# Pooled attention followed by a GELU MLP: the first group in halves, later exps, and the loads on another DMA queue

## The chip, the cores and the metric

The kernel runs on one core of a Trainium2 chip. The metric is the device time of one execution in microseconds (us), lower is better. Engines are named as in the profile: PE (TensorE, matmuls), DVE (VectorE), ACT (ScalarE), POOL (GpSimd) and SP (SyncE, which here only issues DMAs); PEld are the weight loads of PE. The granted clock is the share of PE's full clock that the profile shows as granted. A core has 16 DMA engines; both SP and ACT can issue DMAs, each on a queue of its own.

Executions of a program come in two states, fast and slow. Medians are over all runs. A ratio is the mean time of one kernel's fast runs over that of the other's of the same rounds, so it is not quite the ratio of the medians quoted beside it.

## The reference

```python
# q, k, v: [8 batches, 8 heads, 576 tokens, 64]
k_p = k.reshape(B, H, 72, 8, D).mean(axis=3)      # pooled: 576 keys become 72
v_p = v.reshape(B, H, 72, 8, D).mean(axis=3)
attn = softmax(q @ k_p.T / sqrt(D))
x = (attn @ v_p) as [8*576 tokens, 512]
out = gelu_tanh(x @ w_in) @ w_out                 # w_in [512, 2048], w_out [2048, 512]
```

## The kernel before

The 4608 tokens are nine groups of 512: the first 512 tokens of each of the eight batches, and one group of the 64 tokens left over in each (called R). For each group the MLP is 64 matmuls into the hidden layer and 64 out of it, 512 columns each. The attention of the *next* group is hung into this stream by hooks: `at(s, f)` emits `f` ahead of matmul `s` (0 to 63 hidden, 64 to 127 output). A hook fixes only the order on each engine. An engine that has nothing earlier to do runs its part as soon as its inputs are there.

A steady group (g is the group whose MLP runs, n the next, and the loads are for the one after):

```python
at(0,   pool, dup_k, k_transpose_dma, cast_q, q_transpose_dma)   # DVE, POOL, and DMA transposes on SP's queue
at(30,  loads, seq[n_ + 2])                                      # 3.4 MB of k, v, q, on SP's queue
at(60, 62, 78, 81, scores, n, j)                                 # 4 matmuls and one exp on ACT each
at(79, 81, 85, 89, norm, n, j)                                   # DVE sum, 1/sum; product eb on DVE or POOL
at(79, 81, 85, 89, e_transpose_dma, n, j)                        # eT <- eb, a DMA transpose on SP's queue
at(120, preload gelu table, values, n)                           # 8 matmuls on eT and vbd; ACT copies xT
```

The first group has nothing to hide behind. Its order is: pool K, scores, all four norms, pool V, spread V into the block matrix `vbd` on DVE, PE transposes of the probabilities, values, xT copies, and only then the MLP. The casts of `w_in` run on POOL meanwhile:

```python
norm(0, 3, nc.gpsimd)
pool(0, 5, 9)                    # V, after the softmax
pool(0, 0, 1, 0, 64)
spread_v(0, nc.vector)
[...]
for c in range(4):
    cast_w_in(c, nc.gpsimd)
```

The softmax here doesn't subtract the row's maximum and nothing guards it: scores larger than these inputs give would overflow.

## Time and profile before

| | |
|---|---|
| time | 340.75 us median of 3 (340.33 to 341.77); 341.14 of 4 with the later round |
| span in the profile | 339.6 us |
| first MLP matmul | 37.6 us |
| first MLP matmul of group 1 | 86.7 us |
| from there to the next group's | 31.3, 30.9, 31.2, 31.8, 33.6, 31.4, 30.8 us |

The group starts are read from the timeline of PE: the first matmul that reads `w_in_b` in each group. Two facts set up the argument: before 86.7 us PE idles a lot; after it, the groups follow at about 31 us and PE hardly idles. The prediction below shows the lines. One more view is needed later, the timeline of SP's DMA queue in a steady group (start, length of the issue, queue, line, operation), because the order in it turned out to carry the kernel:

```profile
93.89 1.80 SPq L183 DMA_TRANSPOSE qT<-q_b  x1
95.74 1.14 SPq L97 DMA_DIRECT2D kv<-in_k_dram  x1
...
98.71 0.60 SPq L105 DMA_DIRECT2D q_sb<-in_q_dram  x1
104.72 1.21 SPq L224 DMA_TRANSPOSE eT<-eb  x1
...
108.74 4.26 SPq L224 DMA_TRANSPOSE eT<-eb  x3
```

One queue issues in order: the transpose of q, then the loads, then the transposes of the softmax. The order does not keep them wholly apart: the load of q issued here at 98.71 lands at 109.9, and the four transposes of the softmax land 5.8, 3.1, 2.6 and 2.6 us after their issue. But the last of them, for which the values must wait, meets no load any more, and after group 1's start PE waits for these transposes 1.1 us in all.

### The profile page before, as it was taken

How to read it: one execution, taken by the hardware profiler on the slowest of the kernel's cores; microseconds unless marked ns; L12 is line 12 of the kernel's file. 1: busy time of each engine (PE TensorE's matmuls, PEld its weight loads, DVE VectorE, ACT ScalarE, POOL GpSimd, SP SyncE). 2: the span in 40 equal slices, each digit the busy share in tenths (PEclk: the TensorE clock that was granted, in tenths of full speed). 3: DMA queues.
4: the chain of work that ended last, by engine and by line, in shares of the span. 5: the costliest groups of instructions: out<-in, count | busy, mean ns of one | idle time of the engine just before them, and what ended most of it. 6: DMA issues, size and time to landing. Idle time of an engine off the chain costs nothing. (4 is left out here: it accounts for less than half of the span.)

```text
span 339.6 us, 4031 instructions
## 1 busy us (share of the span) xinstructions
PE 292.8 (86%) x1545; PEld 140.8 (41%) x1545; DVE 133.4 (39%) x193; ACT 171.1 (50%) x237; POOL 73.3 (22%) x68
## 2 busy tenths in 40 slices
PE   5511999092999999999999998999699999999995
PEld 4411544040444444444444443444244454444442
DVE  5488109270606262642446071616162510340011
ACT  1430762040678268446836772685268546926600
POOL 2097225422111320402041113202220400020000
PEclk9555899787899999999999999999999999999999
DMA  7981994599099429926980997299426333162011
GB/s 236 347 313 27 347 348 178 113 315 225 32 236 294 124 65 286 266 102 129 340 187 31 221 283 150 63 296 194 135 72 166 91 122 52 21 129 53 2 62 62
DMA packets 74643, 56.99 MB, mean 168 GB/s; under 512 B 48512, under 2 KB 56704, under 8 KB 74624
## 3 DMA queue, kind: packets, MB, share of 16 engines
q1 hardware_dynamic: 74544, 56.60, 62.5%
q8 instruction: 12, 0.20, 0.2%
q10 hardware_dynamic: 80, 0.13, 0.1%
q14 instruction: 7, 0.06, 0.1%
HBM read 36.70 MB, written 9.44 MB: 136 GB/s over the span
## 5 line engine op out<-in xcount | busy, mean ns | idle before, releaser
L283 PE MATMUL mm<-w_out_b,gT 128*128 128x512 bf16 x576 | 132.5, 382 | 1.6 <-ACT gT L273 1.5
L271 PE MATMUL mm<-xT,w_in_b 128*128 128x512 bf16 x576 | 128.6, 380 | 0.5 <-ACT xT L77 0.5
L273 ACT ACTIVATE gT<-mm 128x512 bf16<-128x512 f32 x144 | 85.9, 597 | 45.2 <-PE mm L271 45.0
L283 PEld LDWEIGHTS <-gT 128*128 128x128 bf16 x576 | 55.7, 98 | 67.5 <-ACT gT L273 3.5
L271 PEld LDWEIGHTS <-w_in_b 128*128 128x128 bf16 x576 | 55.8, 98 | 66.1 <-issue 2.0
L287 DVE COPY osb<-mm 128x512 f32<-128x512 f32 x36 | 24.6, 687 | 92.0 <-PE mm L283 92.0
L211 POOL TENSOR_TENSOR eb<-e,r 128x576 bf16<-128x576 f32 x20 | 23.9, 1198 | 140.0 <-DVE r L210 100.6
L208 DVE TENSOR_REDUCE den<-e 128x8 f32<-128x576 f32 x36 | 26.6, 739 | 66.3 <-ACT e L201 65.5
L77 ACT CAST xT<-xo 128x1024 bf16<-128x1024 f32 x16 | 15.5, 1014 | 48.9 <-PE xo L242 43.8
L201 ACT ACTIVATE e<-sc 128x576 f32<-128x576 f32 x36 | 22.6, 650 | 31.2 <-PE sc L192 15.2
L124 DVE TENSOR_TENSOR kv<-kv 128x2304 f32<-128x2304 f32 (+3 forms) x12 | 23.1, 1926 | 15.8 <-DMA kv<-in_v_dram 13.6
L242 PE MATMUL xo<-eT,vbd 128*128 128x512 bf16 x56 | 14.9, 414 | 11.0 <-DMA eT<-eb 8.3
L135 POOL TENSOR_TENSOR vbd<-kvb,vmask 128x768 bf16<-128x768 bf16 x7 | 10.5, 1499 | 62.2 <-DVE kvb L126 62.2
L192 PE MATMUL sc<-kbd,qT 128*128 128x144 bf16 x128 | 14.6, 244 | 8.7 <-DMA qT<-q_b 7.7
L192 PEld LDWEIGHTS <-qT 128*128 128x128 bf16 x128 | 10.9, 105 | 16.4 <-DMA qT<-q_b 8.2
L79 POOL CAST q_b<-q_sb 128x2048 bf16<-128x2048 f32 x8 | 15.6, 1956 | 5.7 <-issue 4.3
L125 DVE TENSOR_TENSOR kv<-kv 128x1152 f32<-128x1152 f32 (+3 forms) x12 | 15.6, 1300 | 0.4
L211 DVE TENSOR_TENSOR eb<-e,r 128x576 bf16<-128x576 f32 x16 | 14.2, 888 | 0.6
L232 PE MATMUL mm<-eT,vbd 128*128 128x128 bf16 x32 | 3.6, 282 | 12.2 <-DVE vbd L138 12.1
L242 PEld LDWEIGHTS <-vbd 128*128 128x128 bf16 x56 | 5.3, 103 | 19.8 <-issue 7.9
L382 POOL CAST w_out_b<-w_out_s 128x2048 bf16<-128x2048 f32 x4 | 8.0, 2012 | 19.3 <-DMA w_out_s<-in_moe_w_out_dram 19.3
L126 DVE TENSOR_TENSOR kvb<-kv 128x576 bf16<-128x576 f32 (+3 forms) x12 | 11.5, 956 | 0.4
(47 smaller groups left out, 112.6 us busy)
## 6 DMA issues: line engine op xcount, KB each, us to landing
kv<-in_v_dram SPq DMA_DIRECT2D x8, 1024.0 KB, 9.4
out_dram<-osb SPq DMA_DIRECT2D x32, 256.0 KB, 2.5
kv<-in_k_dram SPq DMA_DIRECT2D x7, 1024.0 KB, 7.3
q_sb<-in_q_dram SPq DMA_DIRECT2D x7, 1024.0 KB, 11.4
w_in_s<-in_moe_w_in_dram SPq DMA_DIRECT2D x4, 1024.0 KB, 14.0
w_out_s<-in_moe_w_out_dram SPq DMA_DIRECT2D x4, 1024.0 KB, 13.0
kv<-in_k_dram SPq DMA_DIRECT2D x2, 512.0 KB, 5.2
q_sb<-in_q_dram SPq DMA_DIRECT2D x2, 512.0 KB, 7.4
```

The source lines that it names most:

```text
L79: eng.tensor_copy(out=out, in_=in_)
L124: add(out=t[:, :, 0:4, :], in0=t[:, :, 0:4, :], in1=t[:, :, 4:8, :], op=ALU.add)
L125: add(out=t[:, :, 0:2, :], in0=t[:, :, 0:2, :], in1=t[:, :, 2:4, :], op=ALU.add)
L192: nc.tensor.matmul(out=o, lhsT=qT[:, j, pr, :], rhs=kbd[:, g, pr].rearrange("d hh s -> d (hh s)"), start=True, stop=True)
L201: nc.scalar.activation(out=e.rearrange("p (x h) s -> p x (h s)", x=2), in_=sc[:, :, 0:4 * Sp], func=ACT.Exp, scale=1.0 / 64.0)
L208: nc.vector.reduce_sum(out=den, in_=e, axis=AX.X)
L211: eng.tensor_tensor(out=eb[:, j, 0:W].rearrange("p (h s) -> p h s", s=Sp), in0=e, in1=r.unsqueeze(2).to_broadcast([128, H, Sp]), op=ALU.mult)
L242: nc.tensor.matmul(out=xo[:, i, :], lhsT=vbd[:, g, n, :], rhs=eT[:, :, c, :], start=(x == 0), stop=(x == 1))
L271: nc.tensor.matmul(out=hp, lhsT=w_in_b[:, ko, fo * 128:(fo + 1) * 128], rhs=xT[:, ko, :], start=(ko == 0), stop=(ko == KO - 1))
L273: nc.scalar.activation(out=gT[:, fo, :], in_=hp, func=ACT.Gelu_apprx_tanh)
L283: nc.tensor.matmul(out=ops[i], lhsT=gT[:, fo, (r0 + i) * 128:(r0 + i + 1) * 128], rhs=w_out_b[:, fo, :], start=(fo == 0), stop=(fo == FO - 1))
L287: nc.vector.tensor_copy(out=osb, in_=ops[i])
```

## The change

The intent is to start the MLP of group 0 earlier (half of its tokens first, V pooled before the softmax is normalised, each weight block cast just ahead of its use), to prepare group 1 with PE transposes, to put the exps behind the last gelu so that ACT switches its table twice instead of four times a group, and to take the loads off SP's queue so that the transposes there don't stand behind them. The core of the diff, cut:

```diff
-        e = work.tile([128, H, Sp], F32, name="e")
+        st[g][("sc", j)] = sc
+
+    def exps(g, j):
+        sc = st[g].pop(("sc", j))
+        e = work.tile([128, H, Sp], F32, name="e", bufs=4)
[...]
     load_half(0, "k", nc.scalar)
+    load_half(0, "v", nc.scalar)
[...]
-    pool(0, 1, 3)
[...]
+    pool(0, 0, 3)
[...]
+    pool(0, 5, 7)
+    spread_v(0, nc.gpsimd, (0,))
+    pool(0, 7, 9)
+    norm(0, 0, nc.vector)
+    spread_v(0, nc.gpsimd, (1,))
+    norm(0, 1, nc.vector)
[...]
+    values_half(0, 0, [nc.scalar, nc.vector])
     nc.scalar.preload_act_table_set(GELU_SET)
+    cast_w_in(0, nc.vector)
+    norm(0, 2, nc.gpsimd)
+    norm(0, 3, nc.vector)
+    cast_w_in(1, nc.gpsimd)
+    cast_w_in(2, nc.vector)
+    cast_w_in(3, nc.gpsimd)
[...]
+    at(hooks, 178, loads, 2, nc.scalar)       # end of group 0
[...]
-            t0 = 64 if first else 0
+            t0 = 20
[...]
+                at(hooks, [60, 62, 76, 79][j], scores, n, j)
+                at(hooks, [64, 64, 76, 79][j], exps, n, j)
[...]
-            at(30 if n_ else 100, loads, seq[n_ + 2])
+            at(hooks, 92, loads, seq[n_ + 2], nc.scalar)
```

More of the change, by code (lines that the diff above doesn't have):

```diff
@@ L130, in dup_k, with spread_v, kT_tile @@
         nc.vector.tensor_copy(out=kvb[:, c0:c1, 1, :], in_=kvb[:, c0:c1, 0, :])
-    def spread_v(b, eng):
+    def spread_v(b, eng, parts=(7, 0, 1)):
         kvb = st[b]["kvb"]
         mult = eng.tensor_tensor
-        mult(out=vbd[:, b, 1:7, :].rearrange("p (c r) (hh d) -> p c (r hh) d", c=3, d=D),
-             in0=kvb[:, 6:9, 0, :].unsqueeze(2).to_broadcast([128, 3, 4, D]),
-             in1=vmask[:, 1:4, :].unsqueeze(3).to_broadcast([128, 3, 4, D]), op=ALU.mult)
-        mult(out=vbd[:, b, 0, :].rearrange("p (hh d) -> p hh d", d=D),
-             in0=kvb[:, 5:6, 0, :].to_broadcast([128, 2, D]),
-             in1=vmask[:, 0, 2:4].unsqueeze(2).to_broadcast([128, 2, D]), op=ALU.mult)
-        mult(out=vbd[0:64, b, 7, :].rearrange("p (hh d) -> p hh d", d=D),
-             in0=kvb[0:64, 0:1, 0, :].to_broadcast([64, 2, D]),
-             in1=vmask[0:64, 4, 0:2].unsqueeze(2).to_broadcast([64, 2, D]), op=ALU.mult)
-    def kT_tile(b, ps):
-        if ps:
-            st[b]["kT"] = psum.tile([128, 5 * 128], BF16, name="kT", tag="mm", bufs=4)
+        if 7 in parts:
+            mult(out=vbd[0:64, b, 7, :].rearrange("p (hh d) -> p hh d", d=D),
+                 in0=kvb[0:64, 0:1, 0, :].to_broadcast([64, 2, D]),
+                 in1=vmask[0:64, 4, 0:2].unsqueeze(2).to_broadcast([64, 2, D]), op=ALU.mult)
+        if 0 in parts:
+            mult(out=vbd[:, b, 0, :].rearrange("p (hh d) -> p hh d", d=D),
+                 in0=kvb[:, 5:6, 0, :].to_broadcast([128, 2, D]),
+                 in1=vmask[:, 0, 2:4].unsqueeze(2).to_broadcast([128, 2, D]), op=ALU.mult)
+        if 1 in parts:
+            mult(out=vbd[:, b, 1:7, :].rearrange("p (c r) (hh d) -> p c (r hh) d", c=3, d=D),
+                 in0=kvb[:, 6:9, 0, :].unsqueeze(2).to_broadcast([128, 3, 4, D]),
+                 in1=vmask[:, 1:4, :].unsqueeze(3).to_broadcast([128, 3, 4, D]), op=ALU.mult)
+    BUFS = {"mm": 4, "sc": 2}
+    def kT_tile(b, tag):
+        if tag:
+            st[b]["kT"] = psum.tile([128, 5 * 128], BF16, name="kT", tag=tag, bufs=BUFS[tag])
         else:
@@ L169, in qT_tile, with q_transpose_pe @@
         st[g]["qT"] = work.tile([128, 4, HP, 128], BF16, name="qT", bufs=1)
-    def q_transpose_pe(g, half, eng):
-        tp = psum.tile([128, 4, 2, 128], BF16, name="tp", tag="mm", bufs=4)
+    def q_transpose_pe(g, half, eng, tag):
+        tp = psum.tile([128, 4, 2, 128], BF16, name="tp", tag=tag, bufs=BUFS[tag])
         for i in range(2):
@@ L217, in e_transpose_pe @@
     def e_transpose_pe(g, j, eng):
-        tp = psum.tile([128, 5, 128], BF16, name="tp", tag="sc", bufs=2)
+        tp = psum.tile([128, 5, 128], BF16, name="tp", tag="mm", bufs=4)
         for c in range(5):
@@ L227, in xT_tile, with values_half @@
         st[g]["xT"] = work.tile([128, KO, MAIN], BF16, name="xT")
-    def values_block(g, j, xo):
+    def values_half(g, half, engs):
+        xo = psum.tile([128, HP, 256], F32, name="xo", tag="sc", bufs=2)
         for pr in range(HP):
             for i, (c, n) in enumerate(PARTS[pr]):
-                nc.tensor.matmul(out=xo[pr][:, 128 * j:128 * j + 128], lhsT=vbd[:, g, n, :],
-                                 rhs=st[g]["eT"][:, j, c, :], start=(i == 0), stop=(i == 1))
+                nc.tensor.matmul(out=xo[:, pr, :], lhsT=vbd[:, g, n, :],
+                                 rhs=st[g]["eT"][:, 2 * half:2 * half + 2, c, :], start=(i == 0), stop=(i == 1))
+        for x in range(2):
+            copy(engs[x], st[g]["xT"][:, 2 * x:2 * x + 2, 256 * half:256 * half + 256], xo[:, 2 * x:2 * x + 2, :])
     def values(g, half, eng):
@@ L260, in store, with runner @@
                 nc.sync.dma_start(out=out[r0:r0 + 64, :], in_=osb[64 * half:64 * half + 64])
-    def mlp(g, hooks, nr):
+    def runner(hooks):
         def hook(s):
@@ L265, in hook @@
                 f()
-        xT = st[g]["xT"]
-        for fo in range(FO):
-            hp = psum.tile([128, MAIN], F32, name="mm", tag="mm", bufs=4)
-            for ko in range(KO):
-                hook(4 * fo + ko)
-                nc.tensor.matmul(out=hp, lhsT=w_in_b[:, ko, fo * 128:(fo + 1) * 128], rhs=xT[:, ko, :],
-                                 start=(ko == 0), stop=(ko == KO - 1))
-            nc.scalar.activation(out=gT[:, fo, :], in_=hp, func=ACT.Gelu_apprx_tanh)
-            if fo == FO - 1 and hooks:
-                nc.scalar.preload_act_table_set(EXP_SET)
@@ L276, in mlp @@
-        s = 64
-        for r0 in range(0, 4, nr):
-            ops = [psum.tile([128, DM], F32, name="mm", tag="mm", bufs=4) for _ in range(nr)]
-            for fo in range(FO):
-                for i in range(nr):
-                    hook(s)
-                    s += 1
-                    nc.tensor.matmul(out=ops[i], lhsT=gT[:, fo, (r0 + i) * 128:(r0 + i + 1) * 128],
-                                     rhs=w_out_b[:, fo, :], start=(fo == 0), stop=(fo == FO - 1))
-            for i in range(nr):
-                osb = work.tile([128, DM], F32, name="osb", bufs=4)
-                nc.vector.tensor_copy(out=osb, in_=ops[i])
-                store(g, r0 + i, osb)
+        return hook
@@ new lines, in hidden, with output @@
+    def hidden(g, fo, c0, c1, hook, s):
+        hp = psum.tile([128, MAIN], F32, name="mm", tag="mm", bufs=4)
+        for ko in range(KO):
+            hook(s + ko)
+            nc.tensor.matmul(out=hp[:, 0:c1 - c0], lhsT=w_in_b[:, ko, fo * 128:(fo + 1) * 128],
+                             rhs=st[g]["xT"][:, ko, c0:c1], start=(ko == 0), stop=(ko == KO - 1))
+        nc.scalar.activation(out=gT[:, fo, c0:c1], in_=hp[:, 0:c1 - c0], func=ACT.Gelu_apprx_tanh)
+    def output(g, r, fo, o):
+        nc.tensor.matmul(out=o, lhsT=gT[:, fo, r * 128:(r + 1) * 128], rhs=w_out_b[:, fo, :],
+                         start=(fo == 0), stop=(fo == FO - 1))
@@ new lines, in finish, with mlp @@
+    def finish(g, r, o, eng):
+        osb = work.tile([128, DM], F32, name="osb", bufs=4)
+        copy(eng, osb, o)
+        store(g, r, osb)
+    def mlp(g, hooks, last):
+        hook = runner(hooks)
+        for fo in range(FO):
+            hidden(g, fo, 0, MAIN, hook, 4 * fo)
+        if not last:
+            nc.scalar.preload_act_table_set(EXP_SET)
+        for r in range(4):
+            o = psum.tile([128, DM], F32, name="mm", tag="mm", bufs=4)
+            for fo in range(FO):
+                hook(64 + 16 * r + fo)
+                output(g, r, fo, o)
+            finish(g, r, o, nc.vector)
+        assert not hooks, sorted(hooks)
@@ new lines, in mlp_first @@
+    def mlp_first(g, hooks):
+        hook = runner(hooks)
+        s = 0
+        for half, c in [(0, 0), (0, 1), (0, 2), (1, 0), (0, 3), (1, 1), (1, 2), (1, 3)]:
+            for fo in range(4 * c, 4 * c + 4):
+                hidden(g, fo, 256 * half, 256 * half + 256, hook, s)
+                s += 4
+        nc.scalar.preload_act_table_set(EXP_SET)
+        o = [psum.tile([128, DM], F32, name="mm", tag="mm", bufs=4) for _ in range(4)]
+        for fo in range(12):
+            for r in range(4):
+                hook(s)
+                s += 1
+                output(g, r, fo, o[r])
+        for r in range(4):
+            for fo in range(12, FO):
+                hook(s)
+                s += 1
+                output(g, r, fo, o[r])
+            finish(g, r, o[r], nc.scalar if r == 3 else nc.vector)
@@ L300 @@
     load_q(0, 4, 8, nc.sync)
-    load_main(0, "v", 0, 4, nc.sync)
-    load_half(0, "v", nc.sync)
+    load_main(0, "v", 0, 2, nc.sync)
+    load_main(0, "v", 2, 4, nc.sync)
     nc.scalar.preload_act_table_set(EXP_SET)
@@ L315, in cast_w_in, with w_out_load, cast_w_out @@
         copy(eng, w_in_b[:, :, o:o + 512], w_in_s[c // 2][:, :, 512 * (c % 2):512 * (c % 2) + 512])
+    w_out_s = {}
+    def w_out_load(c):
+        if c % 2 == 0:
+            w_out_s[c // 2] = kvp.tile([128, 8, DM], F32, name="w_out_s", tag="kv")
+        t = w_out_s[c // 2][:, 4 * (c % 2):4 * (c % 2) + 4, :]
+        nc.sync.dma_start(out=t, in_=moe_w_out[512 * c:512 * c + 512, :].rearrange("(fo p) c -> p fo c", p=128))
+    def cast_w_out(c, eng):
+        copy(eng, w_out_b[:, 4 * c:4 * c + 4, :], w_out_s[c // 2][:, 4 * (c % 2):4 * (c % 2) + 4, :])
     make_identity(nc, identb)
@@ L325, with warm_up @@
     nc.gpsimd.memset(vbd[64:128, :, 7, :], 0.0)
-    warm = psum.tile([128, MAIN], F32, name="warm", tag="mm", bufs=4)
-    for _ in range(40):
-        nc.tensor.matmul(out=warm[:, 0:128], lhsT=identb, rhs=identb, start=True, stop=True)
-    kT_tile(0, True)
-    pool(0, 1, 3)
-    dup_k(0, 1, 3)
-    k_transpose_pe(0, 1, 3)
-    pool(0, 0, 1, 64, 128)
-    dup_k(0, 0, 1, 64)
+    def warm_up(n, tag):
+        warm = psum.tile([128, MAIN], F32, name="warm", tag=tag, bufs=BUFS[tag])
+        for _ in range(n):
+            nc.tensor.matmul(out=warm[:, 0:128], lhsT=identb, rhs=identb, start=True, stop=True)
+    warm_up(40, "mm")
+    kT_tile(0, "mm")
+    pool(0, 0, 3)
+    dup_k(0, 0, 3)
+    k_transpose_pe(0, 0, 3)
+    spread_v(0, nc.gpsimd, (7,))
     pool(0, 3, 5)
     dup_k(0, 3, 5)
-    k_transpose_pe(0, 0, 1)
     k_transpose_pe(0, 3, 5)
+    warm_up(12, "mm")
     k_spread(0, [nc.vector, nc.scalar])
@@ L343 @@
     cast_q(0, 0, 4, nc.vector)
-    q_transpose_pe(0, 0, nc.scalar)
+    q_transpose_pe(0, 0, nc.scalar, "mm")
     cast_q(0, 4, 8, nc.vector)
-    q_transpose_pe(0, 1, nc.scalar)
+    q_transpose_pe(0, 1, nc.vector, "mm")
     eT_tile(0)
     xT_tile(0)
-    scores(0, 0)
-    scores(0, 1)
-    norm(0, 0, nc.gpsimd)
-    scores(0, 2)
-    norm(0, 1, nc.gpsimd)
-    scores(0, 3)
-    norm(0, 2, nc.gpsimd)
-    norm(0, 3, nc.gpsimd)
-    pool(0, 5, 9)
-    pool(0, 0, 1, 0, 64)
-    spread_v(0, nc.vector)
@@ L360 @@
-    xo = [psum.tile([128, MAIN], F32, name="mm", tag="mm", bufs=4) for _ in range(HP)]
+    for j in range(4):
+        scores(0, j)
+        exps(0, j)
+    warm_up(24, "mm")
+    pool(0, 5, 7)
[4 more added lines that the diff above has]
+    norm(0, 1, nc.vector)
     e_transpose_pe(0, 0, nc.scalar)
     e_transpose_pe(0, 1, nc.scalar)
-    values_block(0, 0, xo)
-    e_transpose_pe(0, 2, nc.scalar)
-    values_block(0, 1, xo)
@@ L366 @@
-    e_transpose_pe(0, 3, nc.scalar)
-    values_block(0, 2, xo)
-    values_block(0, 3, xo)
-    for pr in range(HP):
-        copy(nc.scalar if pr % 2 else nc.vector, st[0]["xT"][:, pr, :], xo[pr])
-    nc.scalar.preload_act_table_set(GELU_SET)
-    for c in range(4):
-        cast_w_in(c, nc.gpsimd)
-    w_out_s = {}
-    def w_out_load(c):
-        if c % 2 == 0:
-            w_out_s[c // 2] = kvp.tile([128, 8, DM], F32, name="w_out_s", tag="kv")
-        t = w_out_s[c // 2][:, 4 * (c % 2):4 * (c % 2) + 4, :]
-        nc.sync.dma_start(out=t, in_=moe_w_out[512 * c:512 * c + 512, :].rearrange("(fo p) c -> p fo c", p=128))
-        nc.gpsimd.tensor_copy(out=w_out_b[:, 4 * c:4 * c + 4, :], in_=t)
@@ L384, in loads, with first_late @@
-    def loads(n):
+    warm_up(16, "mm")
+    values_half(0, 0, [nc.scalar, nc.vector])
+    nc.scalar.preload_act_table_set(GELU_SET)
+    cast_w_in(0, nc.vector)
[4 more added lines that the diff above has]
+    cast_w_in(3, nc.gpsimd)
+    def first_late():
+        e_transpose_pe(0, 2, nc.vector)
+        e_transpose_pe(0, 3, nc.vector)
+        values_half(0, 1, [nc.vector, nc.vector])
+    w_out_load(0)
+    w_out_load(1)
@@ L385, in loads @@
+    kv_tile(1)
+    q_tile(1)
+    load_main(1, "k", 0, 4, nc.sync)
+    load_half(1, "k", nc.sync)
+    load_half(1, "v", nc.sync)
+    w_out_load(2)
+    load_q(1, 0, H, nc.sync)
+    w_out_load(3)
+    load_main(1, "v", 0, 4, nc.sync)
+    cast_w_out(0, nc.gpsimd)
+    cast_w_out(1, nc.gpsimd)
+    def loads(n, eng):
         q_tile(n)
@@ L388, in loads, with at, tail_of_attention @@
             kv_tile(b)
-            load_main(b, "k", 0, 4, nc.sync)
-            load_half(b, "k", nc.sync)
-            load_main(b, "v", 0, 4, nc.sync)
-            load_half(b, "v", nc.sync)
-        load_q(n, 0, H, nc.sync)
+            load_main(b, "k", 0, 4, eng)
+            load_half(b, "k", eng)
+            load_half(b, "v", eng)
+            load_main(b, "v", 0, 4, eng)
+        load_q(n, 0, H, eng)
+    def at(hooks, s, f, *a):
+        hooks.setdefault(s, []).append(lambda: f(*a))
+    def tail_of_attention(hooks, n, va):
+        at(hooks, va, xT_tile, n)
+        at(hooks, va, nc.scalar.preload_act_table_set, GELU_SET)
+        at(hooks, va, values, n, 0, nc.scalar)
+        at(hooks, va, values, n, 1, nc.scalar)
+    hooks = {}
+    at(hooks, 40, first_late)
+    at(hooks, 127, pool, 1, 0, 5)
+    at(hooks, 127, dup_k, 1, 0, 5)
+    at(hooks, 127, kT_tile, 1, "sc")
+    at(hooks, 127, qT_tile, 1)
+    at(hooks, 130, cast_w_out, 2, nc.gpsimd)
+    at(hooks, 144, k_transpose_pe, 1, 0, 5)
+    at(hooks, 144, k_spread, 1, [nc.vector, nc.scalar])
+    at(hooks, 144, cast_q, 1, 0, 4, nc.vector)
+    at(hooks, 144, cast_q, 1, 4, 8, nc.vector)
+    at(hooks, 158, q_transpose_pe, 1, 0, nc.scalar, "sc")
+    at(hooks, 158, q_transpose_pe, 1, 1, nc.vector, "sc")
+    at(hooks, 158, cast_w_out, 3, nc.gpsimd)
+    at(hooks, 166, eT_tile, 1)
+    for j in range(4):
+        at(hooks, [166, 167, 171, 174][j], scores, 1, j)
+        at(hooks, [166, 167, 171, 174][j], exps, 1, j)
+        at(hooks, [167, 171, 174, 178][j], norm, 1, j, nc.gpsimd if j % 2 else nc.vector)
+        at(hooks, [167, 171, 174, 178][j], e_transpose_dma, 1, j)
+    at(hooks, 178, pool, 1, 5, 9)
+    at(hooks, 178, spread_v, 1, nc.gpsimd)
+    at(hooks, 178, loads, 2, nc.scalar)
+    tail_of_attention(hooks, 1, 191)
+    mlp_first(0, hooks)
     for n_, g in enumerate(seq):
+        if n_ == 0:
+            continue
         hooks = {}
-        def at(s, f, *a):
-            hooks.setdefault(s, []).append(lambda: f(*a))
         if n_ + 1 < len(seq):
@@ L403 @@
             b = B - 1 if n == R else n
-            first = n_ == 0
-            if first:
-                q_tile(n)
-                w_out_load(0)
-                kv_tile(n)
-                load_main(n, "k", 0, 4, nc.sync)
-                load_half(n, "k", nc.sync)
-                load_q(n, 0, H, nc.sync)
-                w_out_load(1)
-                load_main(n, "v", 0, 4, nc.sync)
-                load_half(n, "v", nc.sync)
-                w_out_load(2)
-                w_out_load(3)
@@ L417 @@
-            t0 = 64 if first else 0
-            if n != B - 1:
-                at(t0, pool, b, 0, NB)
-                at(t0, dup_k, b, 0, 5)
-                at(t0, kT_tile, b, False)
-                at(t0, k_transpose_dma, b)
-                at(t0 + 1, spread_v, b, nc.gpsimd)
-                at(t0 + 30, k_spread, b, [nc.vector, nc.vector])
-            at(t0, cast_q, n, 0, H, nc.gpsimd)
-            at(t0, qT_tile, n)
-            at(t0, q_transpose_dma, n)
-            sl = [100, 101, 108, 112] if first else [60, 62, 78, 81]
@@ L429 @@
-            nl = [108, 110, 114, 118] if first else [79, 81, 85, 89]
-            for j in range(4):
-                at(sl[j], scores, n, j)
-            at(nl[0], eT_tile, n)
-            for j in range(4):
-                at(nl[j], norm, n, j, nc.gpsimd if j % 2 else nc.vector)
-                at(nl[j], e_transpose_dma, n, j)
-            va = 127 if first else 120
-            at(va, xT_tile, n)
-            at(va, nc.scalar.preload_act_table_set, GELU_SET)
-            at(va, values, n, 0, nc.scalar)
@@ L440 @@
-            at(va, values, n, 1, nc.scalar)
+            t0 = 20
+            if n != B - 1:
+                at(hooks, t0, pool, b, 0, NB)
+                at(hooks, t0, dup_k, b, 0, 5)
+                at(hooks, t0, kT_tile, b, None)
+                at(hooks, t0, k_transpose_dma, b)
+                at(hooks, t0 + 1, spread_v, b, nc.gpsimd)
+                at(hooks, 58, k_spread, b, [nc.vector, nc.vector])
+            at(hooks, t0, cast_q, n, 0, H, nc.gpsimd)
+            at(hooks, t0, qT_tile, n)
@@ L441 @@
+            at(hooks, t0, q_transpose_dma, n)
+            for j in range(4):
+                at(hooks, [60, 62, 76, 79][j], scores, n, j)
+                at(hooks, [64, 64, 76, 79][j], exps, n, j)
+                if j == 0:
+                    at(hooks, 79, eT_tile, n)
+                at(hooks, [79, 81, 85, 89][j], norm, n, j, nc.gpsimd if j % 2 else nc.vector)
+                at(hooks, [79, 81, 85, 89][j], e_transpose_dma, n, j)
+            tail_of_attention(hooks, n, 120)
         if n_ + 2 < len(seq):
-            at(30 if n_ else 100, loads, seq[n_ + 2])
@@ L443 @@
-        mlp(g, hooks, 4 if n_ == 0 else 1)
+            at(hooks, 92, loads, seq[n_ + 2], nc.scalar)
+        mlp(g, hooks, n_ + 1 == len(seq))
 _INS = ['q', 'k', 'v', 'moe_w_in', 'moe_w_out']
```

## The prediction

> **What bounds the kernel now.** I read the page first, then busy time by stage, then the timeline of the first 90 us and of one steady group, then the waits of PE and the chain that ended last. All times are us from the span's start. The page says that PE is the bound on average, busy 86%, but the second row shows that this is an average of two kernels: a first quarter with holes and a rest without.
>
> ```profile
> span 339.6 us, 4031 instructions
> PE 292.8 (86%) x1545; PEld 140.8 (41%) x1545; DVE 133.4 (39%) x193; ACT 171.1 (50%) x237; POOL 73.3 (22%) x68
> PE   5511999092999999999999998999699999999995
> ```
>
> The stage table (length, then busy us of PE, PEld, DVE, ACT, POOL, granted clock, DMA share, GB/s) gives the holes their size. In order: before the first MLP matmul; the MLP up to a hole; the hole; the rest of group 0; a second hole; values of group 1; one steady group; the steady rest; the tail.
>
> ```profile
> 0.00:37.60 37.60, 15.17 (x129) 12.76 (x130) 24.06 (x35) 9.48 (x14) 16.67 (x20) 0.64 0.73 246
> 37.60:60.50 22.90, 21.98 (x100) 9.69 (x100) 9.22 (x5) 12.36 (x19) 9.14 (x5) 1.00 0.80 262
> 60.50:67.30 6.80, 0.02 (x1) 0.02 (x2) 1.33 (x3) 0.00 (x0) 2.90 (x4) 0.71 0.63 121
> 67.30:75.70 8.40, 8.40 (x43) 4.23 (x43) 5.55 (x11) 3.89 (x5) 1.84 (x2) 0.83 1.02 307
> 75.70:82.90 7.20, 0.01 (x1) 0.04 (x2) 1.49 (x3) 0.00 (x0) 2.35 (x2) 0.83 1.24 231
> 82.90:86.70 3.80, 3.80 (x10) 1.32 (x11) 0.00 (x0) 1.21 (x2) 0.00 (x0) 0.50 0.49 129
> 86.70:118.00 31.30, 31.05 (x154) 14.30 (x153) 13.32 (x20) 19.92 (x27) 6.35 (x6) 0.99 0.71 186
> 118.00:335.50 217.50, 212.38 (x1113) 98.45 (x1111) 77.76 (x119) 124.22 (x172) 34.09 (x32) 1.00 0.56 138
> ```
>
> From 86.7 to 335.5 PE is idle only 0.25 + 5.1 = 5.4 us. So nearly all that can be won lies before 86.7. There the timeline of DVE and POOL names the cause of the longest hole (start, length, then the instruction).
>
> ```profile
> 22.30 1.52 DVE L125 TENSOR_TENSOR kv<-kv 128x512 f32<-128x512 f32 x1
> 23.86 1.99 DVE L126 TENSOR_TENSOR kvb<-kv 128x256 bf16<-128x256 f32 x1
> 25.78 2.10 DVE L124 TENSOR_TENSOR kv<-kv 64x256 f32<-64x256 f32 x1
> 27.91 1.86 DVE L125 TENSOR_TENSOR kv<-kv 64x128 f32<-64x128 f32 x1
> 29.80 1.79 DVE L126 TENSOR_TENSOR kvb<-kv 64x64 bf16<-64x64 f32 x1
> ...
> 23.22 8.30 POOL L79 CAST w_in_b<-w_in_s 128x2048 bf16<-128x2048 f32 x4
> ```
>
> The V pooling comes after the softmax and meets the four weight casts on POOL. A 64x256 add that took 0.42 us at 7.20 takes 2.10 us here, the length of one POOL cast. PE waits 12.1 us for the product, vbd. The waits of PE confirm the three causes, in the order of their size.
>
> ```profile
> PE mm L232 <- DVE vbd L138: 12.1, 1, 12.1
> PE xo L242 <- DMA eT<-eb: 8.3, 3, 7.2
> PE sc L192 <- DMA qT<-q_b: 7.7, 1, 7.7
> ```
>
> **What the Trainium skill says.** (1) "SBUF — State Buffer", section "SBUF: two separate sides": VectorE instructions with two SBUF inputs or in a 2-port mode and GpSimd instructions exclude each other for the whole instruction. The trace agrees: 2.10 us instead of 0.42 us. (2) "TensorE: Matmul & The Clock Gate", section "What's actually happening": the clock is half until about 3.4 us of activity. The trace agrees: granted clock 0.50 until about 36 us, with scores of 144 columns at some 0.15 us each instead of 0.06, and 0.50 again after the hole at 75.7, where eight value matmuls took 3.57 us instead of 1.89. (3) "ScalarE: Activation LUTs", section "What ACT_TABLE_LOAD costs": about 1283 ns plus a drain. The trace shows 1.28 us a load, and four loads in each steady group. (4) "DMA: Bandwidth & Descriptors", section "Queues, rings and completion order": each DMA engine takes packets in turn from the queues that have work. The trace before has hardly two busy queues, so it doesn't show what that does to a transpose.
>
> **The change part by part: the start.** K pooling begins at 5.46 now. It will wait for the half block of V too, second on the ACT queue; I put it at 6.4. Three chunks in one go cost, by 0.16 us plus one element per 1.04 ns (from 128x512 in 0.69 and 128x256 in 0.43), about 0.96 + 0.56 + 0.36 + 0.23 = 2.1, against 1.7 + 1.2 in two goes. With the other two chunks (1.6) K is ready near 10.5; before it was 10.15. Nothing is won here. The second qT copy goes to DVE beside ACT; scores start near 14.6, and four exps, with four e buffers instead of two, end near 18 instead of 19.9. DVE pools V from 14.8: two times 0.69 + 0.43 + 0.29, with gaps and one spread on POOL 3.3, so 18.1. Then two norms of 0.75 + 0.20 + 0.76, the first held back by the 1.5 us spread on POOL: 19.6 + 0.8, then 1.7, so 22.1. Transpose, ACT copy of 0.69: 23.5. Values of the half, xT copies 0.65: 25.5. The first weight cast on DVE, 1.2 (a 128x1024 cast takes 0.64): first MLP matmul near **27.0** instead of 37.6. The DMA page shows that weights cannot be what it waits for: DMA goes quiet at about 24 us now.
>
> **Group 0.** Two halves of 64 matmuls of 256 columns cost the same PE time, 13.9: 144 columns already take 0.0625 each with their weight loads hidden, so 0.108 for 256 is safe. But stalls come in: the second cast waits on POOL behind the third norm, 0.75 + 0.2 + 1.15 + 1.95 = about 4.4 after the first cast, against 1.75 of matmuls: stall 2.7. The late half needs two DVE copies (0.7 each) in mid-stream, its values (0.9) and xT copies: another 2.7. With 0.7 for a cold clock: 20.0, so L283 starts near 47.0 (51.5 before). L283 with transposes and scores of group 1: 13.85 + 2.35 = 16.2, so 63.2. Before it was 24 with the qT hole of 7.7; that hole goes, because q, k and v of group 1 have landed and are transposed by PE. What remains is the end of group 1's softmax: the last scores come 17 matmuls (3.7 us) before the end, and they are followed by exp 0.65, sum 0.75, reciprocal 0.2, product on POOL 1.15, and a transpose of 3.2, with DVE shared among four tiles and the pooling of V. I count 9 us from the last scores, so a wait of **5.5**, instead of 7.2. Values and copy 4.0 (partly cold). First L271 of group 1: 63.2 + 5.5 + 4.0 = **72.7** instead of 86.7. Won: 14.0.
>
> **Steady groups.** The exps move behind the last gelu: two table loads less per group on ACT, and the two waits of PE for a gelu (about 0.28 each) go. The fourth exp no longer waits for an e buffer (1.49 a group). Norms end about as before, since DVE's sums bound them. Of 5.4 us idle I give back 3.5. The tail, 4.1, stays. Span: 72.7 + (248.8 - 3.5) + 4.1 = 322.1. The reported time is 1.2 above the span (340.75 against 339.57): **323**.
>
> **Rivals.** *Loads collide with transposes.* ACT is free after the fourth exp, so its queue starts the 3.4 MB of loads some 19 us into a group, not at matmul 92. They last about 10 us, and in the same time the softmax's transposes run on the other queue. If engines change after every small descriptor, a transpose (640 packets of 256 bytes at 20 ns on 16 engines, 0.8 us) would have a 2 KB packet of 88 ns before each of its own: 4.3 us, and four of them end 5 us after PE wants them. Over six groups that is 30 us: about 350. For it: that page's turn-taking. Against it: a turn may hold several transpose packets, and the old order, the same queue, delayed them too (landing up to 10.5 us). I give it one in ten; a mild form of 1 us a group (329) is more likely. *DVE becomes the bound of the start.* Its work grows to V pooling, both norms, two casts and four copies. If POOL's casts block it again, as above, the first matmul comes at 31 and the second half 3 us later: 329. *Everything fits.* Warm-ups keep the clock at full rate, the first MLP starts at 25, stalls within group 0 are half, wait before group 1 is 2: 314.
>
> **Range and chances.** The mechanism of the start is certain, its sum good to some 5 us; steady state is plus or minus 4, with a tail to slow. I say 314 to 334. Faster by 2% means below 333.9: 0.88. Within 2%: 0.07; slower: 0.05.
>
> **What would show it.** Right: the first L271 at 25 to 29; no wait of PE for vbd; no waits for qT; two table loads a group; the wait for eT ahead of group 1 near 5 us; PE idle below 3 us after group 1 begins. Wrong: steady groups longer than 31.1 us with PE waiting for DMA eT would make the first rival right; DVE adds of 2 us beside POOL casts between 25 and 36 would make the second right.

## The result, and the profile after

The changed kernel takes 370.85 us median (368.04 to 371.84, 4 runs) against 341.14: ratio 1.0859, interval 1.0789 to 1.0929. It is slower by 9%, where 323 us (314 to 334) had been predicted.

The page of the changed kernel, first lines:

```profile
span 368.2 us, 4398 instructions
PE 307.2 (83%) x1666; PEld 152.6 (41%) x1666; DVE 136.2 (37%) x199; ACT 155.3 (42%) x238; POOL 69.5 (19%) x65
PE   4566999159989997499979983999299999999995
```

The holes are no longer only in the first quarter. They recur, one each four slices or so, until near the end. The stage table answers to the one of before: before the first MLP matmul; hidden layer of group 0; its output layer; the hole ahead of group 1; values of group 1; the groups from 1 on, up to the start of the last MLP. Columns: stretch, length, busy us (and instructions) of PE, PEld, DVE, ACT, POOL, granted clock, DMA share, GB/s.

```profile
0.00:29.80 29.80, 15.63 (x147) 13.40 (x147) 16.25 (x28) 8.28 (x11) 4.99 (x14) 0.83 0.96 326
29.80:49.30 19.50, 17.33 (x146) 14.39 (x147) 12.30 (x14) 11.69 (x31) 12.18 (x6) 0.91 0.72 243
49.30:65.50 16.20, 16.16 (x102) 8.22 (x100) 7.32 (x14) 5.76 (x9) 3.04 (x2) 1.00 0.27 83
65.50:77.30 11.80, 0.05 (x1) 0.08 (x2) 6.13 (x8) 0.43 (x1) 4.58 (x4) 0.59 1.12 241
77.30:81.05 3.75, 3.75 (x10) 1.24 (x11) 3.65 (x4) 2.05 (x3) 0.00 (x0) 0.50 1.06 233
81.05:336.70 255.65, 226.71 (x1138) 103.02 (x1137) 87.06 (x131) 117.50 (x170) 44.66 (x39) 0.94 0.56 139
```

The start did win: group 1 begins at 81.0 instead of 86.7. The last MLP begins at 336.5, 255.4 us later; before it was 307.6 - 86.7 = 220.9. So 5.7 us were won and 34.5 lost. Group by group, read from the timelines of PE:

| | first MLP | group 1 begins | from there to the next group's begin |
|---|---|---|---|
| before | 37.6 | 86.7 | 31.3, 30.9, 31.2, 31.8, 33.6, 31.4, 30.8 |
| changed | 29.8 | 81.0 | 35.5, 41.2, 34.9, 40.1, 40.8, 32.1, 30.9 |

The first five of these groups issue the full loads of a later one. The sixth loads only q and the seventh loads nothing, and there the length falls back to 32.1 and 30.9. The waits of PE (us in total, times, longest) say what it waits for:

```profile
PE xo L255 <- DMA eT<-eb: 24.0, 4, 11.8
PE xo L255 <- DMA kv<-in_v_dram: 14.5, 2, 7.3
```

The first line is the wait for the transposed probabilities. The second is put down to a load, but a value matmul reads no load. In the timeline of the second steady group, both queues and the first value matmul:

```profile
136.07 0.37 ACTq L97 DMA_DIRECT2D kv<-in_k_dram  x1
136.48 1.20 SPq L233 DMA_TRANSPOSE eT<-eb  x1
...
139.29 6.55 SPq L233 DMA_TRANSPOSE eT<-eb  x3
145.04 0.37 ACTq L97 DMA_DIRECT2D kv<-in_v_dram  x1
146.69 0.38 ACTq L105 DMA_DIRECT2D q_sb<-in_q_dram  x1
147.10 1.28 ACT L461 ACT_TABLE_LOAD   x1 [10.40 <-DMA eT<-eb]
152.12 1.44 PE L255 MATMUL xo<-eT,vbd 128*128 128x512 bf16 x3 [7.31 <-DMA kv<-in_v_dram]
```

The loads start at 136.07, as soon as ACT has begun its last exp (136.05), and not at matmul 92, behind which the program text has them. The four transposes go out beside them. The last one is issued at 143.0 and lands 9.0 us later, at 152.0; the values start at 152.12. So this wait, too, is for a transpose. The list of DMA issues (times to landing at the end) shows it for all 32, first before, then after:

```profile
eT<-eb SPq DMA_TRANSPOSE x32, 3.2
```

```profile
eT<-eb SPq DMA_TRANSPOSE x32, 7.0
```

For the four of one group, first a group of the kernel before (issued from 166.4), then the group above:

```profile
DMA to landing us min/median/max: 2.6/2.9/5.8
```

```profile
DMA to landing us min/median/max: 6.5/8.0/9.0
```

The last of the four is the one that counts. In the five groups with full loads it lands 4.6, 9.0, 5.0, 9.3 and 9.6 us after its issue, and PE's waits are 2.5, 7.3, 2.7, 7.0 and 7.2 us: the two lists go up and down together. Before, it landed in 2.6 to 3.4 us in all these groups.

ACT is caught as well. Its gelu table load at 147.10 stood 10.40 us idle, behind its own DMA issues, and these waited for a transpose of the other queue. The waits that the compiler built into ACT's program show how. This is an excerpt of the built program, not of the profile, for the first steady group:

```
L97  DMACopy kv<-in_k_dram 128x4x512     [waits DMAHW5,DMAHW1]
L92  DMACopy kv<-in_k_dram 64x512        [waits DMAHW1]
L90  DMACopy kv<-in_v_dram 64x512        [waits DMAHW2]
L97  DMACopy kv<-in_v_dram 128x4x512     [waits DMAHW4]
L105 DMACopy q_sb<-in_q_dram 128x8x256   [waits DMAHW7]
L461 LoadActFuncSet
```

Eight completion counters, DMAHW0 to DMAHW7, go round all DMAs of both queues in program order, and a DMA waits for the last one that had its counter. So a load on ACT's queue can wait for a transpose on SP's, and what ACT has next stands behind it. In the excerpt DMAHW4 and DMAHW7 belong to the first two transposes of the softmax, and the second group is built alike. The trace of that group agrees: its load of v goes out at 145.04, when the first transpose has landed (145.02), and its load of q at 146.69, when the second has (146.67). Yet this hold does not reach PE directly: ACT's table load ends at 148.4, before the values begin at 152.12, and in the whole changed kernel PE waits for ACT about 1 us.

### The profile page after: what moved, and what is told of

Same layout as the page of the kernel before. It is cut to its first block, busy times and chain, and to the rows that moved or that the text cites. A ratio compares the mean times of both kernels' runs of the same rounds, so it can differ in the third digit from the quotient of the medians.

```text
span 368.2 us, 4398 instructions
## 1 busy us (share of the span) xinstructions
PE 307.2 (83%) x1666; PEld 152.6 (41%) x1666; DVE 136.2 (37%) x199; ACT 155.3 (42%) x238; POOL 69.5 (19%) x65
## 5 line engine op out<-in xcount | busy, mean ns | idle before, releaser
L285 PE MATMUL mm<-xT,w_in_b 128*128 128x512 bf16 (+1 forms) x640 | 130.7, 361 | 4.5 <-DVE w_in_b L79 2.5
L287 ACT ACTIVATE gT<-mm 128x512 bf16<-128x512 f32 (+1 forms) x160 | 88.7, 554 | 57.8 <-PE mm L285 56.5
L285 PEld LDWEIGHTS <-w_in_b 128*128 128x128 bf16 x640 | 62.5, 99 | 65.7 <-DVE w_in_b L79 2.8
L255 PE MATMUL xo<-eT,vbd 128*128 128x512 bf16 x56 | 22.4, 570 | 38.7 <-DMA eT<-eb 24.0
L220 POOL TENSOR_TENSOR eb<-e,r 128x576 bf16<-128x576 f32 x17 | 20.3, 1196 | 134.1 <-DVE r L219 122.1
L461 ACT ACT_TABLE_LOAD x8 | 10.3, 1283 | 74.2 <-DMA eT<-eb 55.0
L77 ACT CAST xT<-xo 128x1024 bf16<-128x1024 f32 (+1 forms) x17 | 16.5, 988 | 35.5 <-PE xo L255 25.3
L124 DVE TENSOR_TENSOR kv<-kv 128x2304 f32<-128x2304 f32 (+4 forms) x12 | 21.5, 1795 | 11.7 <-DMA kv<-in_v_dram 6.1
L125 DVE TENSOR_TENSOR kv<-kv 128x1152 f32<-128x1152 f32 (+4 forms) x12 | 15.6, 1304 | 0.4
L197 PEld LDWEIGHTS <-qT 128*128 128x128 bf16 x128 | 9.9, 98 | 11.2 <-issue 3.3
L386 PE MATMUL warm<-identb 128*128 128x128 bf16 x92 | 9.4, 289 | 1.4 <-POOL vmask L375 1.4
L79 DVE COPY kbd<-kTd 64x288 bf16<-64x288 bf16 x12 | 3.1, 258 | 17.9 <-DMA kTd<-kvb 17.9
```

The costliest lines, as they stand in the source:

```text
L77: eng.copy(out=out, in_=in_)
L79: eng.tensor_copy(out=out, in_=in_)
L124: add(out=t[:, :, 0:4, :], in0=t[:, :, 0:4, :], in1=t[:, :, 4:8, :], op=ALU.add)
L125: add(out=t[:, :, 0:2, :], in0=t[:, :, 0:2, :], in1=t[:, :, 2:4, :], op=ALU.add)
L197: nc.tensor.matmul(out=o, lhsT=qT[:, j, pr, :], rhs=kbd[:, g, pr].rearrange("d hh s -> d (hh s)"), start=True, stop=True)
L220: eng.tensor_tensor(out=eb[:, j, 0:W].rearrange("p (h s) -> p h s", s=Sp), in0=e, in1=r.unsqueeze(2).to_broadcast([128, H, Sp]), op=ALU.mult)
```

## The experiments

I had three theories. **A**: the loads and the softmax's transposes are in flight at the same time, and the transposes suffer. **B**: the order of completions is at fault; ACT is held by its DMA issues, whatever they move. **C**: the loads are innocent, and the late exps or the later pooling hook made the groups longer.

### Loads of the steady groups back on SP's queue, same place

```diff
-            at(hooks, 92, loads, seq[n_ + 2], nc.scalar)
+            at(hooks, 92, loads, seq[n_ + 2], nc.sync)
```

> The changed kernel with one word changed: in the groups from 1 on, the loads of the next q, k and v are issued on SP's queue instead of ACT's, at the same matmul 92. On one queue they stand behind the four transposes of the softmax. Theory A (the loads share the 16 DMA engines with those transposes and slow them: landing 7.0 us median instead of 3.2): the groups fall from 35.5 us to about 31.3, six of them, so about 371 - 25 = 346. Theory B (ACT is held: its loads, its gelu table load and its xT copies wait for completions of DMAs on the other queue): the same 346, since ACT issues no loads any more. Theory C (the loads are innocent; the late exps or the later pooling hook at matmul 20 made the groups longer): stays within 3 us of 371.

Measured: 365.06 us against 343.74 of the kernel before, ratio 1.0611. That is only 6 us better by the medians, or 8 by the ratios, not 25. The profile says why; two waits of PE, and the transposes' time to landing:

```profile
PE sc L197 <- DMA qT<-q_b: 19.1, 4, 5.3
...
PE sc L202 <- DMA qT<-q_b: 5.5, 1, 5.5
```

```profile
eT<-eb SPq DMA_TRANSPOSE x32, 2.6
```

The transposes are healed, 2.6 us. But on SP's queue the loads really come after the last of them, and their data now reaches the next group too late: its q is transposed only when the scores should have begun, and PE waits 4 to 5.5 us in five groups. Both A and B missed this; matmul 92 is a bad place on either queue, for two different reasons.

### The loads at the end of group 0 on SP's queue too

```diff
-    at(hooks, 178, loads, 2, nc.scalar)
+    at(hooks, 178, loads, 2, nc.sync)
```

(on top of the edit above)

> As the run before it, and the loads at the end of group 0 on SP's queue too. Theories A and B: the hole of PE ahead of group 1's values (11.8 us in the changed kernel) falls to about 5, so some 6 us below the run before it, about 340. Theory C: no change.

Measured: 364.97 us, ratio 1.0629, no gain over the run before it. Group 1 begins earlier, 73.8 instead of 79.0, since the hole ahead of it fell from 11.2 to 5.0 us, as A and B both say. But then group 1 itself took 38.5 us instead of 31.2, as it now waits for its own late loads. A win in one place was given back at the next.

### As many DMAs on the same queue, with few bytes

From group 3 on each load moves 1/32 of k and v (of their half blocks 1/8) and 1/8 of q, into tiles that group 2 had filled. The result is wrong (relative error 5.0).

```diff
-            kv_tile(b)
+            st[b]["kv"] = st[2]["kv"]           # for n > 2, and q likewise
[...]
-        eng.dma_start(out=st[b]["kv"][:, b0 + c0:b0 + c1], in_=src)
+        eng.dma_start(out=st[b]["kv"][:, b0:b0 + 1, 0:1], in_=src[:, 0:1, 0:1])
```

> Wrong result on purpose. The changed kernel, loads on ACT's queue at matmul 92 with the same number of DMAs and the same waits, but from group 3 on each moves 1/32 (k, v) or 1/8 (q) of its bytes into buffers that group 2 had filled. Theory A (bytes on the shared engines): transposes land in about 3.2 us again, the groups from 2 on fall to about 31.3, five or six of them: about 347. Theory B (order of completions alone holds ACT and SP, bytes don't matter): stays above 360.

Measured: 332.63 us against 343.74, ratio 0.9703. The groups take 31.5, 31.1, 30.9, 31.4, 31.2, 31.6 and 30.9 us, and a transpose lands in 2.9 us. The loads were on ACT's queue, at matmul 92, as many as in the changed kernel. So neither ACT's queue nor the number of DMAs costs anything without the bytes. The waits, however, were not the same, although the expectation had said so: the reused tiles change them, and in the built program of this run the loads of v and q from group 3 on wait for no transpose of the softmax that is under way. So this run alone does not separate the bytes (A) from the crossed waits (B). What speaks against B alone is the trace above: in that group PE waits for the landing of transposes that went out at most 1.4 us after their input was ready, and not for ACT. That the crossed waits also stretch the loads, and so the overlap, remains possible; how much that adds no run here shows.

### This part of the change alone, in the kernel before

```diff
-            at(30 if n_ else 100, loads, seq[n_ + 2])
+            at(92 if n_ else 100, loads, seq[n_ + 2], nc.scalar if n_ else nc.sync)
```

> The kernel before with this part of the change alone: the loads of the steady groups on ACT's queue at matmul 92 instead of SP's at 30; the first group, the exps and the rest as before. Theories A and B: the groups lengthen by 3 to 5 us, six of them: 341 + 18 to 30 = 359 to 371. Theory C: stays within 3 us of 341.

Measured: 382.74 us, ratio 1.1183, even more than expected. Five groups take 37.6 to 41.2 us, transposes land in 7.7 us. The part harms without the rest of the change, so C falls as the main cause.

### Loads on SP's queue at matmul 30

```diff
-            at(hooks, 92, loads, seq[n_ + 2], nc.scalar)
+            at(hooks, 30, loads, seq[n_ + 2], nc.sync)
```

> The changed kernel with the steady loads on SP's queue at matmul 30, as in the kernel before; group 0 with its loads on ACT stays. The two runs with the loads at matmul 92 on SP showed transposes of 2.6 us but data that comes too late for the next group (PE waits 4 to 5 us a group for qT). Theory A', the place in the group decides: a window between the transposes of k and q and those of the softmax is the only one in which 3.4 MB harm nobody. Then the groups fall to about 31 us, and with group 1 starting at 81 the time is 81 + 246 + 5.5 = 333 (ratio 0.975). Theory C (late exps or late pooling cost time): above 345.

Measured: 335.88 us against 340.71, ratio 0.989 (0.98 to 0.9979). The groups take 31.5, 30.9, 31.0, 31.2, 34.0, 31.6 and 31.1 us, transposes 2.8 us. One line undone gives back 33 (by the ratios) to 35 us (by the medians) of 371. The late exps and the hook at matmul 20 are still in this kernel, which settles C.

### The same place on ACT's queue

```diff
-            at(hooks, 92, loads, seq[n_ + 2], nc.scalar)
+            at(hooks, 30, loads, seq[n_ + 2], nc.scalar)
```

> As sp30, but the loads stay on ACT's queue, at matmul 30. Theory A' (place in the group, not the queue): within 1% of sp30, 333 to 336. Theory B (ACT is held while its loads wait for completions, and gelus stand behind them): 5 us or more above sp30, PE waiting for gelus.

Measured: 390.39 us, ratio 1.1418, the slowest of all. (The profiled execution was slow, 395.57; its fast runs are 386.68 to 390.7, so I use only what is far larger than that difference.) The issue list and the waits of PE:

```profile
qT<-q_b SPq DMA_TRANSPOSE x7, 14.4
kTd<-kvb SPq DMA_TRANSPOSE x6, 7.3
```

```profile
PE sc L197 <- DMA qT<-q_b: 30.2, 3, 11.8
PE mm L285 <- ACT gT L287: 19.2, 5, 16.2
```

In the kernel before these two transposes took 4.3 and 2.6 us. "Matmul 30" means something else here. On SP's queue the loads stand behind the transposes of k and q, which the same queue issues first, whenever these get their data. On ACT's queue nothing holds them, so they go at matmul 30 itself and meet just those transposes. The softmax's transposes, whose turn comes later, take 2.6 us. B has its part too: gelus stand behind ACT's loads, and PE waits 19.2 us for them.

### ACT's queue, in the window between the transposes

```diff
-            at(hooks, 92, loads, seq[n_ + 2], nc.scalar)
+            at(hooks, 48, loads, seq[n_ + 2], nc.scalar)
```

> As act30 (390 us) and the changed kernel (371), loads on ACT's queue, but at matmul 48, some 10.5 us into a group, when the transposes of k and q have just gone and those of the softmax are 8 us away. If it is the overlap in time that costs (loads of about 10 us beside transposes on another queue), this should be near sp30: 335 to 345, groups of 31 to 32.5 us. If ACT's queue is bad for loads in itself (gelus held, completions crossed), 365 or more.

Measured: 345.9 us against 341.83, ratio 1.0102. Transposes of all three kinds land in 2.6 to 4.3 us in the median, the last of the softmax in every steady group in 2.6 or 2.7, and the groups take 31.9, 31.5, 31.4, 32.1, 41.1, 31.6 and 30.8 us. So ACT's queue is not bad in itself; the overlap is. The one group of 41.1 us is the one whose loads for R are eight small DMAs. ACT took 9.7 us to issue them, a gelu stood behind, and PE behind the gelu:

```profile
PE mm L290 <- ACT gT L287: 9.0, 1, 9.0
```

This is B, seen once by itself: some 9 us in one group. It is the cost of the issues, and not of a wait for the other queue: in the run with SP's queue at matmul 30 the same eight took 9.71 us to issue as well, but no gelu stands behind SP.

### The loads of group 2 right after those of group 1

```diff
+    loads(2, nc.sync)               # after load_main(1, "v", ...) and two casts
[...]
-    at(hooks, 178, loads, 2, nc.scalar)
[...]
-            at(hooks, 92, loads, seq[n_ + 2], nc.scalar)
+            at(hooks, 30, loads, seq[n_ + 2], nc.sync)
```

> As sp30, and the loads of group 2 moved from the end of group 0 to just after those of group 1, all on SP's queue, where the engines are idle between about 50 and 62 us. Theory A': the hole ahead of group 1's values falls from 11.8 to about 4, so some 7 us below sp30: 326 (ratio 0.955). If instead the hole is made by the softmax chain itself, it stays above 9 and the time equals that of sp30.

Measured: 328.83 us against 340.71, ratio 0.9656 (0.9571 to 0.9741), a correct kernel faster than both. The hole ahead of group 1 in its stage table, to be held against the 11.80 us above:

```profile
65.80:70.80 5.00, 0.00 (x0) 0.02 (x1) 4.93 (x7) 0.00 (x0) 4.31 (x4) 0.96 0.67 103
```

PE idles 5.0 us here, and DVE and POOL are busy nearly all of it with V's pooling and spread. The values start at 70.81, when the last transpose has landed; its product on POOL took 1.95 us beside that pooling. That is the wait that the prediction had put at 5.5.

### The late exps alone, in the kernel before

```diff
+    def exps(g, j):                                   # four e buffers, as in the change
[...]
-            sl = [100, 101, 108, 112] if first else [60, 62, 78, 81]
+            sl = [100, 101, 108, 112] if first else [60, 62, 76, 79]
+            el = [100, 101, 108, 112] if first else [64, 64, 76, 79]
```

> The kernel before with this part alone: exps behind the last gelu in the steady groups, four e buffers. My prediction: two waits of PE for a gelu go, 0.3 us each at most, so 1 to 3 us off 341 (ratio 0.991 to 0.997). Theory C (this part made the groups longer): ratio above 1.02.

Measured: 340.55 us against 340.71, ratio 0.9993 (0.9932 to 1.0053): nothing. ACT loads a table 18 times instead of 32, some 18 us less of its time at 1.28 each, and PE's waits for gelus are gone. But the groups take 31.3, 30.9, 31.2, 31.4, 33.9, 31.6 and 30.8 us as before. ACT was not the bound.

### Two edits of the start

On top of the kernel of 328.8 us: K's chunks pooled as they come and V's half block later; the first two weight casts on POOL while it idles; both.

```diff
-    pool(0, 0, 3)                      # k_first
+    pool(0, 1, 3) [...] pool(0, 0, 1, 64, 128) [...] pool(0, 3, 5); later pool(0, 0, 1, 0, 64)
```

```diff
     spread_v(0, nc.gpsimd, (1,))       # casts_pool
+    cast_w_in(0, nc.gpsimd)
+    cast_w_in(1, nc.gpsimd)
```

> sp30_early2 (328.8) with one part of the start undone: K's chunks are pooled as they come and the half block of V later, with V. My prediction let all of K wait for V's half until 6.4 us; in the profile of the changed kernel that wait ends at 8.64, against 5.46 in the kernel before. If this wait is what made the start late, K is ready 2 us earlier, the first MLP matmul comes near 28 instead of 30, and the time falls by 1 to 2 us: 327. If something later sets the start (q, V), no change.

> sp30_early2 with the first two casts of the first weights on POOL right after V's spread, while POOL is idle (21 to 31 us), instead of after the norms. They exclude a DVE product for up to 2 us, but the first MLP matmul no longer waits for a cast on DVE (1.2) nor the second chunk for one on POOL (1.3): 2 to 3 us less than sp30_early2, 326. If DVE loses as much at the second norm as is won, no change.

> sp30_early2 with both of the edits of the two runs before it: 3 to 4 us below sp30_early2, 325 (ratio to the kernel before 0.953), if the two gains lie on one chain and add up.

Measured, against 341.83: 327.88 (ratio 0.9573), 328.89 (0.9615) and 328.61 (0.9596). The intervals overlap each other and that of 0.9656, so none of the three is shown to gain. In the first, K's pooling starts at 5.34 instead of about 8.6 and the first MLP matmul comes at 28.6. But in the profiles of the eight kernels that share the unedited start it comes anywhere from 28.2 to 30.2, so this gain is not shown either. The hidden layer of group 0 then took 21.6 us at a granted clock of 0.80, where the 328.8 us kernel took 19.5 at 0.93. An earlier start does not bring the colder clock: the run with few bytes started at 29.2 and had the same (0.80, 21.6 us), and the one with SP's queue at matmul 30 started at 28.2 and had 0.91 and 19.5 us. With the two casts on POOL the first MLP matmul came at 27.0, earlier than in any of the eight, but the time did not show it.

## Why the prediction was wrong

It was wrong by one term of the sum, the steady groups, and by the weight given to a rival that it had named.

- **Failed: the term of the steady groups, "(248.8 - 3.5)".** From the begin of group 1 to the last osb copy it is 364.3 - 81.0 = 283.3 us, 38 more than the 245.3 of the sum. The step that broke is the one that left the loads out of that sum. I had seen that ACT's queue would start the loads when the fourth exp is done, beside the transposes, and still gave it one chance in ten, among other things because "the old order, the same queue, delayed them too". That was the fault in reasoning. In the old order the loads did delay the first transposes of a group's softmax (up to 7.1 us to landing), but they were through before the last one was issued, and PE waits for the last. Six runs show it: loads beside transposes cost 30 to 50 us against the kernel before in the three places where they overlapped them in the groups with full loads (371, 383, 390), 4 us where they mostly missed them on the same ACT queue (346), and nothing on SP's queue at matmul 30 (336) or with few bytes, though with other waits (333).
- **The rival's size.** Its 4.3 us a transpose, 5 us late at the end of a group, 350 in all, had the right direction and was too small: groups grew by up to 10.3 us (41.2 against 30.9). It took the loads to last about 10 us. They lasted longer, since their own issues waited for transposes through the shared completion counters: in the group shown above the first went out at 136.07 and the last at 146.69, to land at 156.0. And it left the colder clock out: after such a hole the eight value matmuls took 3.57 us instead of 1.89. Its mechanism, one load packet ahead of each transpose packet, is not shown. In the middle of such an overlap (139.5 to 142.5 us) the trace has 514 packets of SP's queue and 264 of ACT's. Nor can it be the whole of it: of the 2560 packets of that group's four transposes (256 bytes each) the first starts at 140.8, 4.3 us after the first issue, and the last at 147.7, but the last transpose lands at 152.0, another 4.3 us later. In the three groups in which PE waited 7 us the landing came 4.2 to 4.3 us after the last packet, in the two in which it waited under 3 us, and in the steady groups of the kernel before, 0.5 to 0.7 us. So the longest waits were in part for the word of completion, after the packets had gone. What in the DMA engines holds it back I leave open.
- **The start: mechanism right, 2.8 us short.** 27.0 was predicted and 29.8 came (28.2 to 30.2 in the eight profiles with this start). K's pooling waited for V's half block until 8.64 us instead of 6.4; how much of the 2.8 us this makes is not shown. The prediction's "granted clock 0.50 until about 36 us" was misread for the first 8 us, where the trace shows 1.00. DVE never met POOL's casts before the first MLP; the 12.1 us wait for vbd is gone, as predicted.
- **Inside group 0: the sums right, one of them by luck.** Hidden layer 19.5 (20.0 predicted); output layer 16.2 (16.2); values and copy 3.75 (4.0). But in the hidden layer the MLP matmuls were busy 16.1 us instead of 13.9 + 0.7, at a granted clock of 0.67 in the first 5.2 us, and the second cast cost PE 1.2 us instead of 2.7 (the terms given for it add up to 4.05 us, not 4.4). Two errors cancelled. The wait of 2.5 us for the first cast comes ahead of the first MLP matmul.
- **The hole ahead of group 1: 11.8 instead of 5.5.** Again the loads: with them out of the way it is 5.0.
- **Late exps: 1 to 3 us expected in that step, 0.2 measured, within the noise.** PE's waits for gelus did go, but not the groups' length.
- The tail, 4.1 predicted, is 3.9.

With the loads left where they had been, the sum would have been near: 335.9 measured, and 328.8 with the early loads of group 2, against 323 predicted.

## What to carry to other kernels

A single DMA queue is also a schedule: here its order had the large loads through before the small transfer that PE waits for last, and moving the loads to another queue dropped that order, even though the program text reads much the same. Before such a move, ask when the other engine will really reach the issue, what is in flight then, and who waits for it; a DMA put behind a matmul in the text went out here as soon as its engine had nothing else to do. And an expected gain from a large load's new place must be counted twice: what it meets in flight, and when its data is needed.

## What the Trainium skill lacked or had wrong

- "DMA: Bandwidth & Descriptors", section "Rules for kernel authors", says that a transpose next to ordinary DMAs needs nothing. That may hold for its correctness, as all kernels but one gave the right result. It lacks the price: beside loads of 3.4 MB on the other queue, transposes landed in 7.0 us in the median instead of 3.2 (eT), in 14.4 instead of 4.3 (qT) and in 7.3 instead of 2.6 (kTd).
- No page that I read says that the built program shares eight completion counters among all DMAs of both queues in program order, so that a DMA on one queue waits for one on the other. In the changed kernel ACT stood idle 10.40 us in the group shown, behind two loads that waited so. (The 9.0 us that PE lost with the loads at matmul 48 on ACT's queue are another thing: the plain cost of eight issues on an engine that computes.)
